# From unit 12 on, k and r are turned by VectorE in blocks of 32 and put in place by DMAs

## The chip, the cores and the metric

The kernel runs on one core of one Trainium2 chip. A core has the engines TensorE (PE in the profile, with its weight loads as PEld), VectorE (DVE), ScalarE (ACT), GpSimd (POOL) and SyncE (SP, which here only issues DMAs), and 16 DMA engines. SBUF is the on-chip memory of 128 partitions; PSUM is where TensorE writes. The metric is device time in microseconds of one execution; lower is better.

## The reference

Inputs are r, k and v of shape (batch 4, heads 8, positions 768, head size 48), a decay w and a bonus u per head and channel, and three feed-forward weights. All is 32-bit floating point.

```
for t in range(768):
    y[t]  = r[t] @ (state + (u * k[t]) outer v[t])      # per batch and head
    state = w * state + k[t] outer v[t]
x   = y, laid out as (4*768, 8*48) = (3072, 384)
g   = x @ w_gate            # 384 -> 1536
out = (g * sigmoid(g) * (x @ w_val)) @ w_out            # 1536 -> 384
```

## The kernel before

**Units.** The 3072 tokens are cut into 24 units of 128 tokens. Unit i is chunk c = i // 4 of batch b = i % 4, so four neighbouring units are the same chunk of the four batches. For a unit the recurrence becomes matrix products. k times powers of the decay is khat and r times their inverse is rhat; the product of the two, turned so that channels lie on the partitions (kT and rT), gives a 128x128 score per head. A mask keeps the scores of earlier positions, the bonus term stands on the diagonal (At), and the outputs are At times v plus rT times the state Z that the earlier chunks left. The update adds khat times v to Z.

**The steps of a unit.** `load` and `load_v` fetch k, r and v through SP's queue. `scale(i)` makes khat and rhat on POOL (L289, L293), and `own_product` the bonus products there (L211, L212), summed by DVE in `own_sum` (L217). `turn(i)` is eight transposes on PE, for the four pairs of heads of khat and then of rhat, into PSUM (L322), and two ACT copies to SBUF, kT (L324) and rT (L327). `diagonal` writes At on ACT (L309), `scores` runs PE (L335) and two masked copies on DVE (L340), `outputs` runs PE (L365) and an ACT copy into xT (L369), `update` PE (L378), DVE (L391) and POOL (L392).

**Buffers.** khat has four buffers (unit i uses i % 4), rhat two (i % 2), each of 128 partitions x 8 heads x 64 columns, of which 48 hold data and 16 zeros. kT has two, rT three. xT keeps the x of NX = 12 units in a ring.

**The feed-forward part.** Units are handled in groups of four by `four_units`: sums of x and of weights are made beforehand, so that 11 products per column block f do the work of more (L580, accumulators c_a and c_b in PSUM). The steps p1, p6 and p7 copy c_a to SBUF buffers of the ring "part" by ACT (L587, named p, u2 and u3), and DVE (L589 to L596) and POOL (L540 to L543, L564) combine them into hT. `two_projections` then multiplies hT by w_out (L474), and ACT issues the output stores (L497). These products are cut into some 40 pieces a group.

**The order.** It is written out by hand: each engine executes its instructions in the order in which the program names them, and semaphores are set for every dependence. The loop over stages s holds, in this order: own_sum(s); scale(s+1), own_product(s+1), load_v(s+1), load(s+3); turn(s); pieces; scores(s-1); from stage 12 on outputs(s-2); pieces; pieces; diagonal(s); pieces; update(s-2); pieces. `gaps(s, n)` feeds the pieces: from stage 12 on a stage takes its share of what is queued, at most 14, and divides it over the five places. A new group is queued every fourth stage, so a stage takes between 3 and 14 pieces.

**The names that matter here.** `scale_k`, `scale_r`, `turn`, `scores`, `outputs`, the ring "part" (pool `seven`), xT with NX, and the loop over s (L757 on).

Of the kernel before, what the change touches and what calls it, by code (L numbers as in the profile page):

```python
# [9 lines left out]
FP32 = mybir.dt.float32  # L10
# [5 lines left out]
P = 128  # L16
# [6 lines left out]
def fast(  # L23
# [25 lines left out]
    B, H, S, D = r.shape  # L49
    D2 = 2 * D  # L50
    VW = 2 * D + 16
    HP = H // 2
    R2 = 64 + D
    NCH = S // P
    N = B * NCH
# [3 lines left out]
    cst = ctx.enter_context(tc.tile_pool(name="cst", bufs=1))  # L59
    one = ctx.enter_context(tc.tile_pool(name="one", bufs=1))  # L60
    two = ctx.enter_context(tc.tile_pool(name="two", bufs=2))
    three = ctx.enter_context(tc.tile_pool(name="three", bufs=3))
    seven = ctx.enter_context(tc.tile_pool(name="seven", bufs=7))
    ps_a = ctx.enter_context(tc.tile_pool(name="ps_a", bufs=4, space=bass.MemoryType.PSUM))
    ps_w = ctx.enter_context(tc.tile_pool(name="ps_w", bufs=1, space=bass.MemoryType.PSUM))
    ps_f = ctx.enter_context(tc.tile_pool(name="ps_f", bufs=2, space=bass.MemoryType.PSUM))
# [7 lines left out]
    rscale = cst.tile([P, H, D], FP32, name="rscale")  # L74
# [9 lines left out]
    wg = cst.tile([P, CC, DFF], FP32, name="wg")  # L84
    wv = cst.tile([P, CC, DFF], FP32, name="wv")
    wo = cst.tile([P, FC, DM], FP32, name="wo")
    NX = 12
    xT = cst.tile([P, NX, CC, P], FP32, name="xT")
    Z = [cst.tile([P, HP, D2], FP32, name=f"Z{b}") for b in range(B)]
    r_ld = [cst.tile([P, H, D], FP32, name=f"r_ld{i}") for i in range(2)]  # L90
# [2 lines left out]
    v_ld = [cst.tile([P, HP, VW], FP32, name=f"v_ld{i}") for i in range(4)]  # L93


    khat = [cst.tile([P, H, 64], FP32, name=f"khat{i}") for i in range(4)]
    rhat = [cst.tile([P, H, 64], FP32, name=f"rhat{i}") for i in range(2)]
    At = [cst.tile([P, H, P], FP32, name=f"At{i}") for i in range(2)]
    kT = [cst.tile([P, HP, P], FP32, name=f"kT{i}") for i in range(2)]

    def load(i):
        c, b = divmod(i, B)
# [117 lines left out]
    sg0 = two.tile([P, 1], FP32, name="sg0", tag="sg0")  # L220
    for t in v_ld:
        dve.memset(t[:, :, D:64], 0.0)
    for t in khat + rhat:
        dve.memset(t[:, :, D:64], 0.0)
    dve.memset(wcol[:], 1.0)
    for e in range(2):
        sp.dma_start(out=wcol[64 * e : 64 * e + D, :], in_=w.rearrange("(a e) d -> e d a", e=2)[e])
# [57 lines left out]
    turned = {}  # L285
    small = deque()

    def scale_k(i):
        pool.tensor_mul(khat[i % 4][:, :, 0:D], k_ld[i % 2][:], kscale[:])  # L289

    def scale_r(i):
        for h in (slice(0, HP), slice(HP, H)) if i == 0 else (slice(0, H),):
            pool.tensor_mul(rhat[i % 2][:, h, 0:D], r_ld[i % 2][:, h], rscale[:, h])  # L293

    def scale(i):
        scale_k(i)
# [21 lines left out]
    def turn(i):  # L318
        for nm, t in (("kT", khat[i % 4]), ("rT", rhat[i % 2])):
# [5 lines left out]
            else:  # L325
                turned[i] = three.tile([P, HP, P], FP32, name=nm, tag=nm)
                act.copy(turned[i][:], tp[:])  # L327

    def scores(i):

        ps = [ps_a.tile([P, HP, P], FP32, name="s_ps", tag="a") for _ in range(2)]
        for a in range(HP):
            for e in range(2):
                rows = slice(64 * e, 64 * e + D)
                pe.matmul(  # L335
                    ps[e][:, a, :], kT[i % 2][rows, a, :], turned[i][rows, a, :],
                    start=True, stop=True, skip_group_check=True,
                )
        for e in range(2):
            dve.copy_predicated(  # L340
                At[i % 2][:].rearrange("p (a e) t -> p a e t", e=2)[:, :, e],
                mask[:].bitcast(INT32).unsqueeze(1).to_broadcast([P, HP, P]), ps[e][:],
            )

    def outputs(i):

        c, b = divmod(i, B)
        A, vl, z = At[i % 2], v_ld[i % 4], Z[b]  # L350
        rT = turned.pop(i)
        ps = ps_a.tile([P, CC, P], FP32, name="y_ps", tag="a")
        cols = [[] for _ in range(4)]
        for m in range(4 * CC):
            (cc, q), (a, s) = divmod(m, 4), divmod(m, 3)
            each = [(z[0:R2, a, 32 * s : 32 * s + 32], rT[0:R2, a, :])] if c > 0 else []
            if s < 2:
                each.append((vl[:, a, 32 * s : 32 * s + 32], A[:, 2 * a, :]))
            if s > 0:
                each.append((vl[:, a, 32 * s + 16 : 32 * s + 48], A[:, 2 * a + 1, :]))  # L360
            cols[q] += [(cc, x, n == 0, n == len(each) - 1) for n, x in enumerate(each)]
        for n in range(len(cols[0])):
            for q in range(4):
                cc, x, start, stop = cols[q][n]
                pe.matmul(  # L365
                    ps[32 * q : 32 * q + 32, cc, :], *x,
                    start=start, stop=stop, skip_group_check=True,
                )
        act.copy(xT[:, i % NX, :, :], ps[:])  # L369

# [82 lines left out]
    def project(g, n):  # L453

        h11, h12, h21, h22 = h_quarters(g)
        x = part_of.setdefault(g, {})
        if n == 0:
            one_bank = ps_f.tile([P, 2, 2 * P], FP32, name="o_f", tag="gv")[:, 0, 0:NH]
            if g % 2 == 0:
                x["a"] = ps_o.tile([P, 2 * P], FP32, name="o_a", tag="o")[:, 0:NH]  # L460
                x["b"] = one_bank
            else:
                x["a"] = one_bank
                x["b"] = ps_w.tile([P, 2 * P], FP32, name="o_b", tag="w_mag")[:, 0:NH]
            x["out"] = [two.tile([P, DM], FP32, name=n, tag=n) for n in ("o_sb1", "o_sb2")]
        lhs, rhs, acc = (
            (h11, w11, "a"), (h12, w21, "b"), (1, wt[0], "a"), (2, wt[1], "a"),
            (0, w12, "b"), (h22, wt[2], "a"), (3, w22, "b"),
        )[n]
        if isinstance(lhs, int):  # L470
            lhs = x["s"][lhs]
        ps = x[acc]
        for f in range(FH):
            pe.matmul(  # L474
                ps, lhs[:, f, :], rhs[:, f, :],
                start=(f == 0 and n in (0, 1, 4)), stop=(f == FH - 1), skip_group_check=True,
            )
        o1, o2 = x["out"]
        if n in (0, 2, 3):
            nm = {0: "p1", 2: "u2", 3: "u3"}[n]  # L480
            x[nm] = seven.tile([P, 2 * P], FP32, name=nm, tag="part")[:, 0:NH]
            act.copy(x[nm], ps)
        elif n == 1:
            dve.tensor_add(o1[:, 0:NH], x["p1"], ps)
        elif n == 5:
            act.copy(o2[:, 0:NH], ps)
        elif n == 6:
            dve.tensor_add(o1[:, NH:DM], x["u2"], ps)  # L488
        if n in (3, 4):
            if "c22" in x:  # L490
                dve.tensor_add(o2[:, NH:DM], x["u3"], x["b"])
            x["c22"] = True
        if n >= 5:
            j = 6 - n
            c, b = divmod(2 * g + j, B)
            n0 = S * b + P * c
            act.dma_start(out=out[n0 : n0 + P, :], in_=x["out"][j][:])  # L497
# [47 lines left out]
    def four(g, f, what):  # L545
# [37 lines left out]
        )  # L583
        if what in ("p1", "p6", "p7"):
            nm = {"p1": "p1", "p6": "u2", "p7": "u3"}[what]
            x[nm, f] = seven.tile([P, 2 * P], FP32, name=nm, tag="part")
            act.copy(x[nm, f][:], ps)  # L587
        elif what == "c11":
            dve.tensor_add(h[0], x.pop(("p1", f))[:], ps)  # L589
        elif what == "c21":  # L590
            dve.tensor_mul(h[0], h[0], x.pop(("sg0", f))[:])
            dve.tensor_mul(h[0], h[0], ps)
        elif what == "c22":
            dve.tensor_add(x["u3", f][:], x["u3", f][:], ps)  # L594
        elif what == "c12":
            dve.tensor_add(h[1], x.pop(("u2", f))[:], ps)  # L596
# [59 lines left out]
    def gaps(s, n):  # L656

        if s not in EARLY:
            if n == 0:
                share[0] = min(-(-len(todo) // (4 - (s - 9) % 4)), 14)  # L660
            feed(share[0] // 5 + (n < share[0] % 5))
            return
        for what in EARLY[s][n]:
            if what == "R":
                if done["pool"] < NW:
                    round_weights()
                elif len(summed) < 4:
                    weight_sum()
            else:
                feed(1)  # L670

    share = [0]
    LATE = 12
    EARLY = {s: ("" if s < 7 else "R", "F", "R", "F", "RF") for s in range(5, 12)}
    EARLY[4] = ("R", "F", "", "F", "F")
# [81 lines left out]
    for s in range(4, N + 2):  # L757
        if 4 < s < N:
            own_sum(s)
        if s + 1 < N:  # L760
            scale(s + 1)
            own_product(s + 1)
            load_v(s + 1)
            if s + 3 < N:
                load(s + 3)
        if s < N:
            turn(s)
        gaps(s, 0)
        if 4 <= s - 1 < N:
            while small:  # L770
                small.popleft()()
            scores(s - 1)
            if s >= LATE:
                outputs(s - 2)
            gaps(s, 1)
        gaps(s, 2)
        if s - 2 >= 4 and (s < LATE or s > N):
            outputs(s - 2)
        if s >= 5 and s % 2:
            queue((s - 3) // 2)  # L780
        if s < N:
            diagonal(s)
        if s - 2 >= 4:
            gaps(s, 3)
            update(s - 2)
        gaps(s, 4)
        if s == 12:
            n_ps = ps_a.tile([P, HP, P], FP32, name="n_ps", tag="a")
            pe.matmul(n_ps[0:1, 0, 0:1], badc[:], ones[:], start=True, stop=True)
            act.copy(outside, n_ps[0:1, 0, 0:1])  # L790
# [417 lines left out]
```

## Time and profile before

| What | Value |
|---|---|
| Median of 3 runs | 655.1 us (655.0 to 655.13) |
| Profiled execution, its own time | 655.57 us |
| Its span, first to last instruction | 653.5 us |
| Granted TensorE clock, mean | 0.996 |
| PE, PEld busy | 98%, 88% of the span |
| DVE, ACT, POOL busy | 53%, 39%, 46% |
| Turns on PE, units 0 to 23 | 192, from 13.9 to 459.2 us |
| The turns of units 12 to 23 begin at | 140.4, 169.5, 189.1, 227.5, 261.3, 292.4, 309.1, 346.0, 373.8, 412.6, 424.5, 458.4 us |
| ACT copies of turns, kT and rT | 24 of 578 ns and 24 of 593 ns |

A line of the groups reads: line of the kernel, engine, operation, what it writes and reads, shape, count, busy us, mean ns. The timeline has the start in us, the duration of a merged run of instructions, and what they are; an entry in brackets is the idle time of the engine ahead of it and what ended that. The durations of matmuls overlap, so their cost is read from start to start.

### The profile page before, as it was taken

What the parts mean: (1) busy time and instruction counts of PE and PEld (TensorE: products, weight loads), DVE (VectorE), ACT (ScalarE), POOL (GpSimd) and SP (SyncE); (2) the same over time, 40 slices, a digit from 0 to 9 for tenths busy, and PEclk for the clock granted to TensorE, in tenths of its full rate; (3) what the DMA queues carried; (4) which work ended last, traced back from release to release, by engine and by line L of the source; (5) the groups of instructions that cost most, each with busy time, mean ns of one, the idle gap of its engine ahead of it and who ended that gap; (6) DMA issues with size and microseconds to landing.
All of it is one profiled execution on the core that took longest, in us unless ns stands there. A gap on an engine that the chain in (4) does not pass through costs nothing.

```text
span 653.5 us, 11994 instructions
## 1 busy us (share of the span) xinstructions
PE 637.3 (98%) x4702; PEld 575.2 (88%) x4702; DVE 348.8 (53%) x711; ACT 257.4 (39%) x686; POOL 300.2 (46%) x333
## 2 busy tenths in 40 slices
PE   8899998999999999999999999999999999999996
PEld 8787877899988889988889988889988889988896
DVE  6668888364365556256548145546245546255460
ACT  4557776431344431344432244451244430234310
POOL 5968777961854430836416534641334310534110
PEclk9899999999999999999999999999999999999999
DMA  8969784221210010201101210000000000100001
GB/s 192 253 151 214 224 212 98 41 38 39 70 38 1 14 25 24 62 13 38 25 1 38 60 26 2 13 14 2 25 26 1 0 2 12 38 0 2 2 1 53
DMA packets 85779, 34.10 MB, mean 52 GB/s; under 512 B 76369, under 2 KB 79569, under 8 KB 85713
## 3 DMA queue, kind: packets, MB, share of 16 engines
q1 hardware_dynamic: 82256, 28.52, 19.0%
q10 hardware_dynamic: 3456, 4.72, 2.0%
q8 instruction: 39, 0.64, 0.4%
q14 instruction: 28, 0.22, 0.1%
HBM read 28.51 MB, written 4.72 MB: 51 GB/s over the span
## 4 chain that ended last, share of the span: by engine, by line
PE 86%; DVE 8%; ACT 4%; issue 1%; DMA 0%; SPq 0%; DVEq 0%; ACTq 0%
PE c_b L580 24%; PE c_a L580 20%; PE o_f L474 13%; PE o_a L474 7%; PE o_b L474 5%; PE y_ps L365 5%; PE gv L403 4%; PE s_ps L335 3%; PE tp L322 2%; PE u_ps L378 2%; ACT At L309 2%; DVE At L340 1%; DVE wo L184 1%; PE warm L245 1%; DVE hT L411 1%
## 5 line engine op out<-in xcount | busy, mean ns | idle before, releaser
L564 POOL TENSOR_TENSOR hT<-hT,u 128x256 f32<-128x256 f32 x60 | 47.3, 788 | 187.9 <-DVE hT L563 160.9
L587 ACT COPY u<-c_a 128x256 f32<-128x256 f32 x120 | 44.6, 371 | 87.0 <-PE c_a L580 86.9
L580 PE MATMUL c_a<-t,wv 128*128 128x256 f32 x240 | 72.0, 382 | 0.2 <-ACT u L587 0.2
L580 PE MATMUL c_b<-xT,wg 128*128 128x256 f32 x240 | 71.7, 380 | 0.0
L560 ACT ACTIVATE sg<-hT 128x256 f32<-128x256 f32 x120 | 50.0, 417 | 50.5 <-DVE hT L589 31.5
L309 ACT ACTIVATE At<-ident,du 128x128 f32<-128x128 f32 x184 | 64.3, 397 | 9.4 <-DVE o_sb L488 7.7
L594 DVE TENSOR_TENSOR u<-u,c_b 128x256 f32<-128x256 f32 x60 | 25.3, 421 | 70.4 <-PE c_b L580 64.1
L580 PE MATMUL c_b<-xT,s 128*128 128x256 f32 x240 | 61.6, 379 | 0.0
L589 DVE TENSOR_TENSOR hT<-p,c_b 128x256 f32<-128x256 f32 x60 | 25.2, 421 | 48.7 <-ACT u L587 24.4
L580 PEld LDWEIGHTS c_b<-xT,s 128*128 128x128 f32 x240 | 45.2, 190 | 6.6 <-DVE u L594 0.3
L540 POOL TENSOR_TENSOR s<-wv,wg 128x256 f32<-128x256 f32 x24 | 17.6, 733 | 72.4 <-PE o_f L474 57.1
L580 PEld LDWEIGHTS c_a<-t,wv 128*128 128x128 f32 x240 | 44.6, 190 | 7.1 <-ACT u L587 1.2
L580 PEld LDWEIGHTS c_b<-xT,wg 128*128 128x128 f32 x240 | 45.0, 190 | 6.1 <-issue 0.4
L340 DVE COPY_PREDICATED At<-mask,s_ps 128x512 f32<-128x512 int32 x48 | 33.0, 744 | 26.2 <-ACT At L309 16.0
L403 PE MATMUL gv<-xT,wg 128*128 128x256 f32 x144 | 36.8, 392 | 3.4 <-DVE hT L411 3.4
L365 PE MATMUL y_ps<-At,v_ld 128*32 128x128 f32 x768 | 36.1, 278 | 2.8 <-DVE At L340 2.8
L580 PE MATMUL c_b<-t,s 128*128 128x256 f32 x120 | 36.2, 383 | 0.0
L596 DVE TENSOR_TENSOR hT<-u,c_b 128x256 f32<-128x256 f32 x60 | 25.2, 421 | 20.1 <-PE c_b L580 19.9
L580 PE MATMUL c_b<-xT,wv 128*128 128x256 f32 x120 | 35.9, 381 | 0.0
L580 PE MATMUL c_a<-t,s 128*128 128x256 f32 x120 | 35.8, 380 | 0.0
L580 PE MATMUL c_a<-xT,wg 128*128 128x256 f32 x120 | 35.8, 380 | 0.0
L580 PE MATMUL c_a<-xT,wv 128*128 128x256 f32 x120 | 35.7, 379 | 0.0
(133 smaller groups left out, 1425.7 us busy)
## 6 DMA issues: line engine op xcount, KB each, us to landing
k_ld<-in_k_dram SPq DMA_DIRECT2D x24, 192.0 KB, 3.6
r_ld<-in_r_dram SPq DMA_DIRECT2D x24, 192.0 KB, 3.8
w_bits<-in_moe_w_gate_dram SPq DMA_DIRECT2D x6, 768.0 KB, 6.2
v_ld<-in_v_dram SPq DMA_DIRECT2D x48, 96.0 KB, 3.1
w_bits<-in_moe_w_val_dram SPq DMA_DIRECT2D x6, 768.0 KB, 6.5
w_bits<-in_moe_w_out_dram SPq DMA_DIRECT2D x6, 768.0 KB, 4.5
out_dram<-o_sb ACTq DMA_DIRECT2D x24, 192.0 KB, 1.9
ub<-in_u_dram SPq DMA_DIRECT2D x1, 192.0 KB, 4.1
```

The costliest lines, as they stand in the source:

```text
L309: lambda h=h: act.activation(At[i % 2][:, h, :], ident[:], AF.Identity, scale=du[:, h : h + 1])
L340: dve.copy_predicated(At[i % 2][:].rearrange("p (a e) t -> p a e t", e=2)[:, :, e], mask[:].bitcast(INT32).unsqueeze(1).to_broadcast([P, H ...
L365: pe.matmul(ps[32 * q : 32 * q + 32, cc, :], *x, start=start, stop=stop, skip_group_check=True,)
L403: pe.matmul(gv[:, o, :].rearrange("p (i t) -> p i t", i=2), wt[:, c, P * f : P * (f + 1)], xT[:, 2 * g % NX : 2 * g % NX + 2, c, :], start ...
L474: pe.matmul(ps, lhs[:, f, :], rhs[:, f, :], start=(f == 0 and n in (0, 1, 4)), stop=(f == FH - 1), skip_group_check=True,)
L560: act.activation(x[what, f][:], h[j], AF.Sigmoid)
L564: pool.tensor_mul(h[1], h[1], x.pop(("u3", f))[:])
L580: pe.matmul(ps.rearrange("p (i t) -> p i t", i=2), lhs, rhs, start=first, stop=what not in ("p2", "p5", "p4", "p3"), skip_group_check=True,)
L587: act.copy(x[nm, f][:], ps)
L589: dve.tensor_add(h[0], x.pop(("p1", f))[:], ps)
L594: dve.tensor_add(x["u3", f][:], x["u3", f][:], ps)
L596: dve.tensor_add(h[1], x.pop(("u2", f))[:], ps)
```

## The change

From unit 12 on PE no longer turns khat and rhat. A full turn of a 128x128 matrix is done in two steps instead: DMAs inside SBUF move 32x32 blocks to their mirrored places (16 DMAs a unit, each with 32 partitions x 8 pairs x 32 columns, issued by SP), and DVE turns each 32x32 block where it lies, once for kT and once for rT, straight to SBUF. khat and rhat become slots of one tile `hats` with two more slots for the moved blocks. The slots are arranged so that the k and the r of a unit are neighbours; for that, from unit 12 on two neighbouring units share one rhat buffer (i % 4 // 2), and the pairs of heads of even units lie in reversed order, which `at` undoes in `scores` and `outputs`. The DMAs of unit s+1 and the DVE turn of unit s are named in stage s after the second group of pieces. To make room, xT keeps 10 units, and the ring "part" has six buffers.

```diff
-    seven = ctx.enter_context(tc.tile_pool(name="seven", bufs=7))
+    six = ctx.enter_context(tc.tile_pool(name="six", bufs=6))
...
-    NX = 12
+    NX = 10
...
-    khat = [cst.tile([P, H, 64], FP32, name=f"khat{i}") for i in range(4)]
-    rhat = [cst.tile([P, H, 64], FP32, name=f"rhat{i}") for i in range(2)]
+    hats = cst.tile([P, 8, H, 64], FP32, name="hats")
+    khat, rhat = [hats[:, n] for n in (0, 2, 3, 5)], [hats[:, n] for n in (1, 4)]
...
+    blocks = [hats[:, n].rearrange("p h x -> p (h x)") for n in (7, 6)]
...
-    for t in khat + rhat:
-        dve.memset(t[:, :, D:64], 0.0)
+    dve.memset(hats[:, 0:6, :, D:64], 0.0)
...
+    def rhat_of(i):
+        return rhat[i % 2 if i < BLOCKS else i % 4 // 2]
+
+    def at(i, a):
+        return HP - 1 - a if i >= BLOCKS and i % 2 == 0 else a
...
+    def move_blocks(i):
+        h = hats[:].rearrange("p n h x -> p (n h x)")
+        first, step = ((0, 1), (11, -1), (12, 1), (23, -1))[i % 4]
+        for m in range(4):
+            for q in range(4):
+                src = h[32 * q : 32 * q + 32, P * first + 32 * m : P * first + 32 * m + 1]
+                dst = h[32 * m : 32 * m + 32, P * 31 + 32 * q : P * 31 + 32 * q + 1]
+                sp.dma_start(
+                    out=bass.AP(
+                        tensor=dst.tensor, offset=dst.offset,
+                        ap=[list(dst.ap[0]), [-P, 2 * HP], [1, 32]],
+                    ),
+                    in_=bass.AP(
+                        tensor=src.tensor, offset=src.offset,
+                        ap=[list(src.ap[0]), [P * step, 2 * HP], [1, 32]],
+                    ),
+                )
+
+    def turn_blocks(i):
+        turned[i] = three.tile([P, HP, P], FP32, name="rT", tag="rT")
+        for dst, src in ((kT[i % 2], blocks[0]), (turned[i], blocks[1])):
+            dve.transpose(dst[:].rearrange("p a t -> p (a t)"), src)
...
-                    ps[e][:, a, :], kT[i % 2][rows, a, :], turned[i][rows, a, :],
+                    ps[e][:, a, :], kT[i % 2][rows, at(i, a), :], turned[i][rows, at(i, a), :],
...
+    BLOCKS = 12
...
-        if s < N:
+        if s < BLOCKS:
             turn(s)
...
             gaps(s, 1)
+        if BLOCKS <= s < N:
+            turn_blocks(s)
+        if BLOCKS <= s + 1 < N:
+            move_blocks(s + 1)
         gaps(s, 2)
```

More of the change, by code (lines that the diff above doesn't have):

```diff
@@ L292, in scale_r @@
         for h in (slice(0, HP), slice(HP, H)) if i == 0 else (slice(0, H),):
-            pool.tensor_mul(rhat[i % 2][:, h, 0:D], r_ld[i % 2][:, h], rscale[:, h])
+            pool.tensor_mul(rhat_of(i)[:, h, 0:D], r_ld[i % 2][:, h], rscale[:, h])
     def scale(i):
@@ L355, in outputs @@
             (cc, q), (a, s) = divmod(m, 4), divmod(m, 3)
-            each = [(z[0:R2, a, 32 * s : 32 * s + 32], rT[0:R2, a, :])] if c > 0 else []
+            each = [(z[0:R2, a, 32 * s : 32 * s + 32], rT[0:R2, at(i, a), :])] if c > 0 else []
             if s < 2:
@@ L480, in project @@
             nm = {0: "p1", 2: "u2", 3: "u3"}[n]
-            x[nm] = seven.tile([P, 2 * P], FP32, name=nm, tag="part")[:, 0:NH]
+            x[nm] = six.tile([P, 2 * P], FP32, name=nm, tag="part")[:, 0:NH]
             act.copy(x[nm], ps)
@@ L585, in four @@
             nm = {"p1": "p1", "p6": "u2", "p7": "u3"}[what]
-            x[nm, f] = seven.tile([P, 2 * P], FP32, name=nm, tag="part")
+            x[nm, f] = six.tile([P, 2 * P], FP32, name=nm, tag="part")
             act.copy(x[nm, f][:], ps)
```

## The prediction

> **What bounds the kernel now.** I read the page first: busy time by engine, then the chain that ended last. The columns of the first line are busy us, share of the span, instructions.
>
> ```profile
> PE 637.3 (98%) x4702; PEld 575.2 (88%) x4702; DVE 348.8 (53%) x711; ACT 257.4 (39%) x686; POOL 300.2 (46%) x333
> ...
> PE 86%; DVE 8%; ACT 4%; issue 1%; DMA 0%; SPq 0%; DVEq 0%; ACTq 0%
> PE c_b L580 24%; PE c_a L580 20%; PE o_f L474 13%; PE o_a L474 7%; PE o_b L474 5%; PE y_ps L365 5%; PE gv L403 4%; PE s_ps L335 3%; PE tp L322 2%; PE u_ps L378 2%; ACT At L309 2%; DVE At L340 1%; DVE wo L184 1%; PE warm L245 1%; DVE hT L411 1%
> ```
>
> TensorE carries the chain, and the turns (tp) are 2% of it. A share is an average, so I took the table of busy time in stretches, one per stage from stage 12 on (columns: length, PE, weight load, DVE, ACT, POOL, granted clock).
>
> ```profile
> 189.00:228.00 39.00, 39.00 (x251) 34.07 (x250) 22.39 (x50) 17.75 (x50) 21.22 (x27) 1.00 0.10 19
> 292.00:309.00 17.00, 17.00 (x147) 14.87 (x146) 11.53 (x21) 7.54 (x21) 11.24 (x15) 1.00 0.16 32
> 413.00:425.00 12.00, 12.00 (x125) 10.51 (x124) 6.39 (x14) 5.31 (x15) 7.08 (x9) 1.00 0.00 1
> ```
>
> PE fills every such stretch; over 140 to 460 us its records leave 0.2 us idle. There a microsecond taken from PE is a microsecond of the kernel, unless a wait takes its place. Stages are unequal, 12 to 39 us, because the planner feeds different numbers of feed-forward pieces; this decides below.
>
> **What is removed.** The mean of 273 ns for a turn overlaps its neighbours, so I took the timeline of PE at unit 14's turn (start, us, then the group).
>
> ```profile
> 189.12 0.60 PE L322 MATMUL tp<-ident,khat 128*128 128x128 f32 x4
> 189.55 0.60 PE L322 MATMUL tp<-ident,rhat 128*128 128x128 f32 x4
> 189.99 0.60 PE L580 MATMUL c_b<-xT,wg 128*128 128x256 f32 x2
> ```
>
> From the first turn to the next product is 0.87 us; eleven of the twelve units from 12 on show 0.87, one 0.93. So 12 x 0.87 + 0.06 = **10.5 us** leave PE. ACT loses 24 copies of about 0.585 us (14 us); worth nothing, since PE does not wait for it here. Without this cover the gain would not exist at all: it is only PE's time that counts.
>
> **What is added, and its prices.** *DVE.* Two block turns of 128x512 per unit. The trace has none. [...] I take 0.69 because the masked copies of the same shape (L340) take 0.74. DVE is 53% busy and has room. The pair stands in DVE's program order behind the second group of pieces, and what is queued behind it are sums that free PE's accumulators. The tight one is L589: it runs from 302.57 to 302.99, 0.6 us before PE writes its accumulator again. A pair just ahead holds it up to 1.4 us less the idle 0.6 us, which costs PE up to 0.4 us. One unit in three or four meets that: 3 x 0.35 = **1.0 us**. Ends: 0, and 12 x 1.4 = 17 us if nothing were covered.
>
> *SP and the transfers.* 16 issues a unit, 32 KB each in 256 runs of 128 B, 192 issues in all. [...] q1's 82256 packets took 19.0% of 16 engines' 653.5 us, 24 ns each[...]. Issuing takes longer. From the source view of the v loads, minimum, median and maximum in ns, and the time to landing:
>
> ```profile
> L111 SPq DMA_DIRECT2D v_ld<-in_v_dram x48: 367/498/2253, 8.2 to 425.1; - x48
> ...
> DMA to landing us min/median/max: 2.0/3.1/6.5
> ```
>
> The first of a pair is 0.37, the second 0.50, and the first loads at start-up follow each other by 0.46 to 0.62. So 15 x 0.47 + 1.9 (the page's row of the output stores, from issue to landing) = 9.0 us from the first issue to the last landing. Call it X; bounds 7.5 (0.37 an issue) and 14 (every issue as slow as 0.58, with 0.2 of waits between and landing 2 us). [...] in the trace's wait fields loads and stores take eight completion semaphores in turn and each waits for the one before on its own. Eight issues span 3.8 us against some 2 us of landing, so that adds nothing inside a unit.
>
> **Where it waits.** move_blocks(s+1) needs scale(s+1), done at the top of stage s, and turn_blocks(s), since it overwrites the blocks. So it starts in mid-stage and has until the next mid-stage: 12 us or more, above X, so DVE does not wait. Loads queue behind it on SP for up to 7 us; they are wanted a stage or two later, so nothing.
>
> POOL does wait. For units from 12 on, two neighbours share one rhat buffer, so scale_r of odd i must wait until move_blocks(i-1) has landed, and those have only the rest of a stage. What is queued behind it on POOL is seen in its timeline at the top of stage 14:
>
> ```profile
> 189.94 0.99 POOL L293 TENSOR_TENSOR rhat<-r_ld,rscale 128x384 f32<-128x384 f32 x1
> 190.90 0.99 POOL L211 TENSOR_TENSOR rk<-r_ld,k_ld 128x384 f32<-128x384 f32 x1
> 191.97 1.07 POOL L212 TENSOR_TENSOR rk<-rk,ub 128x384 f32<-128x384 f32 x1
> 192.99 0.73 POOL L564 TENSOR_TENSOR hT<-hT,u 128x256 f32<-128x256 f32 x1
> ```
>
> L564 releases a "part" buffer, ACT fills it next with a copy of c_a, and PE needs that copy before it adds to c_a again. By the wait fields buffers are handed out in the order of their release: with seven, the u2 copies wait for POOL; with six it is the next copy, p, at 194.16 here. It starts 0.44 us after L564 ends (2.3 us usually), and PE has 0.6 us more; the turn taken away brings it 0.87 us nearer. So six buffers alone cost nothing, but a late POOL reaches PE. Unit by unit:
> - 15: moves start about 183.0 (stage 13's second group ends near 181.2, the pair follows), scale_r is due at 189.94, so it is X-6.9 late; PE stalls X-6.9 + 0.87 - 0.44 - 0.6 = X-7.1.
> - 19: moves start 303.5, due 309.72; L564 would end at 313.54, its copy is due 315.4 plus 0.6; PE stalls X-8.7.
> - 23: moves start 422.9, due 427.29; the copy comes late, at 436.77 before; PE stalls X-9.8.
> - 13, 17, 21: X-7.7, none, X-11 late, in stages where the copies have 2 us or more.
> At X = 9.0: 1.9 + 0.3 = **2.2 us**.
>
> *ACT.* Its output stores share the eight semaphores. A store behind the moves can wait for a move and hold ACT: the stores at 160.4, 162.4, 275.3 and 364.1 lie near moves. If the shared semaphore's last holder is an early move the cost is 0, if a late one some 4 us at 275.3, where products follow. I take **0.5 us**.
>
> *The rest.* x for 10 units: a slot is rewritten ten units on, and the group that reads it has then been through PE for a stage or more: 0. One memset of 768 columns replaces six of 128 (165 ns): 0. The reversed order of pairs (at) changes addresses only. [...]
>
> **The sum.** Profiled span 653.5 - 10.5 + 1.0 + 2.2 + 0.5 = 646.7 us. The profiled execution took 655.57, 2.07 around its span, and the median of the runs is 655.1, 0.47 below; so 646.7 + 1.6 = 648.3, and I say **648.5 us**.
>
> **Rivals.**
> - *A, the sum above*: 645.5 to 652. For it: PE full, X computed from issue rows.
> - *B, all hidden*: X at 7.5 and the DVE pair in gaps; 655.1 - 10.5 + 0.4 = 645.0. Against it: the short stages 13 and 21.
> - *C, the transfers become the bound through POOL, slower than before*: the stalls are 3X - 25.6, and with 1.5 for the rest they reach 10.5 at X = 11.5; at 13.5 the time is 655.1 - 10.5 + 1.5 + 14.9 = 661.0. This needs 0.64 us an issue, or a wait between DMAs that the trace does not show. For it: r loads hold SP 0.58, and 128 B runs between partitions are in no row. Against it: those r loads follow 1024 runs, these 256.
> - *D, ACT held by shared semaphores[...]*: 3 x 2.5[...] = 8 us on top of 2; 652 to 657. That scale_k or the updates wait for moves because all lie in one tile would give the same; against it, xT is one tile too and PE read it at 320.75 while ACT still wrote another part.
>
> **Chances.** A 0.46, B 0.12, C 0.27, D 0.15. The measurement can tell 0.2%, about 1.3 us. A and B are faster; D splits in thirds; C is slower: faster 0.63, same 0.05, slower 0.32. A's own range is 645.5 to 652; for 8 in 10 the range takes in B and C up to X = 13.5: 644.5 to 661.5.
>
> **What the next profile shows.** Right: tp only to unit 11; PE still over 97% busy; 192 more issues on SP at about 0.47; turns near 0.7 us; POOL L293 waiting for a DMA at the tops of stages 12, 14, 18 and 22, by 2, 3 and 5 us in the last three, and PE idle after ACT copies of c_a in 14. Wrong: moves over 11 us from first issue to landing, DVE waiting for a DMA at the turns, ACT waiting at a store, or an idle PE at other tops than these.

## The result and the profile after

The changed kernel takes **644.52 us** (median of 6 runs, 643.26 to 645.14) against 654.92 us before (median of 6, 654.05 to 655.13): ratio 0.984, interval 0.9828 to 0.9853. The forecast was 648.5 us; the gain is 10.4 us instead of 6.6. The time lies where rival B stood (645.0), below the range of the sum itself (645.5 to 652) and at the very edge of the wide one (644.5 to 661.5).

The page of the changed kernel, in the order in which the page of before was read: span, busy us by engine (share, instructions), the chain that ended last by engine and by line, the group of `scale_r` on POOL (busy us, mean ns | idle before it and what ended it), the DMA queue q1 (packets, MB, share of 16 engines), and the new DMA issues (KB each, us to landing).

```profile
span 641.6 us, 12075 instructions
...
PE 625.3 (97%) x4606; PEld 563.7 (88%) x4606; DVE 361.6 (56%) x730; ACT 245.1 (38%) x662; POOL 300.2 (47%) x333
...
q1 hardware_dynamic: 134480, 34.82, 25.7%
...
PE 83%; DVE 8%; ACT 4%; issue 2%; DMA 1%; SPq 1%; POOL 0%; DVEq 0%; ACTq 0%
PE c_b L615 24%; PE c_a L615 20%; PE o_f L509 13%; PE o_a L509 7%; PE o_b L509 6%; PE y_ps L400 5%; PE gv L438 3%; PE s_ps L370 3%; ACT At L318 2%; PE u_ps L413 2%; DVE wo L187 1%; DVE hT L446 1%; DMA w_bits<-in_moe_w_gate_dram 1%; DVE sg L445 1%; DVE wo L188 1%
...
L302 POOL TENSOR_TENSOR hats<-r_ld,rscale 128x384 f32<-128x384 f32 (+1 forms) x25 | 25.0, 1001 | 24.1 <-DMA hats<-hats 24.1
...
hats<-hats SPq DMA_DIRECT2D x192, 32.0 KB, 2.0
```

PE has 96 instructions fewer and 12.0 us less of busy time in this execution; tp is no longer among the lines of the chain. DVE has 12.8 us more, and POOL now waits 24.1 us for the moves. Yet PE is still busy 97% of a shorter span. Lines have moved: L580 is now L615, L587 is L622, L564 is L599, L293 is L302; the moves are L347, the block turns L362.

The table of busy time in stretches, for the same three stages as in the prediction (each stretch shorter by about the turn that is gone; columns as there):

```profile
185.60:223.70 38.10, 37.99 (x239) 32.99 (x238) 21.98 (x50) 16.81 (x48) 21.27 (x27) 1.00 0.26 43
286.30:302.40 16.10, 16.10 (x138) 13.89 (x138) 12.28 (x22) 6.23 (x19) 11.16 (x15) 1.00 0.23 40
403.80:414.90 11.10, 11.10 (x116) 9.61 (x115) 7.54 (x16) 4.31 (x13) 6.92 (x9) 1.00 0.05 7
```

PE fills the stages as it did: over 140 to 460 us its records leave 0.21 us idle, against 0.2 before. The timeline of PE at the place of unit 14's turn shows the seam closed, 0.43 us from start to start:

```profile
185.36 0.59 PE L615 MATMUL c_a<-xT,wv 128*128 128x256 f32 x2
185.79 0.59 PE L615 MATMUL c_b<-xT,wg 128*128 128x256 f32 x2
```

Where the gain arises is seen when one product is followed through both traces, the first product of a unit's outputs (y_ps), in us from the start of the span. The second execution is the run e0 below, of the same kernel.

| y_ps, before | after | later or earlier | e0_changed | later or earlier |
|---|---|---|---|---|
| 78.14 | 76.54 | -1.60 | 77.69 | -0.45 |
| 133.28 | 131.66 | -1.62 | 132.84 | -0.44 |
| 148.31 | 145.82 | -2.50 | 147.00 | -1.31 |
| 236.91 | 232.13 | -4.77 | 232.98 | -3.93 |
| 353.89 | 345.64 | -8.25 | 346.49 | -7.40 |
| 466.31 | 454.48 | -11.83 | 455.33 | -10.97 |
| 527.15 | 515.32 | -11.83 | 516.18 | -10.97 |

Between 133.28 and 466.31 the distance grows by 10.21 us in one execution and 10.53 us in the other, and neither before nor after. From one stage to the next it grows by 0.8 to 1.0 us; only once, in the first execution ahead of the y_ps at 232.13, it is 0.5. The constant 1.6 or 0.44 us lies at the start-up, differs between two executions of one kernel, and is not the change's. So the twelve turns are gained whole in e0_changed; in the other execution 0.3 us is given back at one place, which is shown under e3.

### The profile page after: what moved, and what is told of

Its sections match the earlier page's. It is cut to its first block, busy times and chain, and to the rows that moved or that the text cites. A ratio compares the mean times of both kernels' runs of the same rounds, so it can differ in the third digit from the quotient of the medians.

```text
span 641.6 us, 12075 instructions
## 1 busy us (share of the span) xinstructions
PE 625.3 (97%) x4606; PEld 563.7 (88%) x4606; DVE 361.6 (56%) x730; ACT 245.1 (38%) x662; POOL 300.2 (47%) x333
## 4 chain that ended last, share of the span: by engine, by line
PE 83%; DVE 8%; ACT 4%; issue 2%; DMA 1%; SPq 1%; POOL 0%; DVEq 0%; ACTq 0%
PE c_b L615 24%; PE c_a L615 20%; PE o_f L509 13%; PE o_a L509 7%; PE o_b L509 6%; PE y_ps L400 5%; PE gv L438 3%; PE s_ps L370 3%; ACT At L318 2%; PE u_ps L413 2%; DVE wo L187 1%; DVE hT L446 1%; DMA w_bits<-in_moe_w_gate_dram 1%; DVE sg L445 1%; DVE wo L188 1%
## 5 line engine op out<-in xcount | busy, mean ns | idle before, releaser
L599 POOL TENSOR_TENSOR hT<-hT,u 128x256 f32<-128x256 f32 x60 | 47.5, 793 | 162.2 <-DVE hT L598 135.2
L622 ACT COPY u<-c_a 128x256 f32<-128x256 f32 x120 | 44.5, 371 | 87.2 <-PE c_a L615 86.9
L615 PE MATMUL c_a<-t,wv 128*128 128x256 f32 x240 | 72.2, 382 | 0.1
L615 PE MATMUL c_b<-xT,wg 128*128 128x256 f32 x240 | 71.7, 380 | 0.0
L615 PE MATMUL c_b<-xT,s 128*128 128x256 f32 x240 | 61.6, 379 | 0.0
L615 PEld LDWEIGHTS c_b<-xT,s 128*128 128x128 f32 x240 | 45.3, 190 | 6.6 <-DVE u L629 0.2
L615 PEld LDWEIGHTS c_a<-t,wv 128*128 128x128 f32 x240 | 44.7, 190 | 7.0 <-ACT u L622 1.1
L615 PEld LDWEIGHTS c_b<-xT,wg 128*128 128x128 f32 x240 | 45.2, 190 | 6.2 <-issue 0.4
L624 DVE TENSOR_TENSOR hT<-p,c_b 128x256 f32<-128x256 f32 x60 | 25.1, 419 | 42.9 <-PE c_b L615 39.9
L615 PE MATMUL c_b<-t,s 128*128 128x256 f32 x120 | 36.2, 383 | 0.1
L302 POOL TENSOR_TENSOR hats<-r_ld,rscale 128x384 f32<-128x384 f32 (+1 forms) x25 | 25.0, 1001 | 24.1 <-DMA hats<-hats 24.1
L627 DVE TENSOR_TENSOR hT<-hT,c_a 128x256 f32<-128x256 f32 x60 | 25.3, 421 | 19.1 <-PE c_a L615 18.0
L615 PE MATMUL c_b<-xT,wv 128*128 128x256 f32 x120 | 35.9, 381 | 0.0
L615 PE MATMUL c_a<-t,s 128*128 128x256 f32 x120 | 35.8, 380 | 0.0
```

The lines of the kernel that those rows point to most:

```text
L599: pool.tensor_mul(h[1], h[1], x.pop(("u3", f))[:])
L615: pe.matmul(ps.rearrange("p (i t) -> p i t", i=2), lhs, rhs, start=first, stop=what not in ("p2", "p5", "p4", "p3"), skip_group_check=True,)
```

## The experiments

Two theories stood at first. **H**: the gain is PE's time of the 96 turns, and everything added is hidden. **K**: the additions cost about what was forecast (3.7 us), and some other part of the change, the single tile, the six buffers or x for ten units, gains as much. Each edit is made to the changed kernel; ratios are against the kernel before.

| Run | Edit | us | Ratio, interval |
|---|---|---|---|
| e0_changed | none | 644.38 | 0.9839 (0.9826 to 0.9853) |
| e1_pe_turns | PE turns all units | 655.13 | 1.0004 (0.9995 to 1.0012) |
| e2_no_turns | no turn at all from unit 12 | 645.77 | 0.986 (0.9845 to 0.9875) |
| e6_act_copies | ACT's 24 copies are back | 645.54 | 0.9863 (0.9847 to 0.9878) |
| e3_dve_twice | block turns doubled | 650.45 | 0.9931 (0.9917 to 0.9944) |
| e9_four_moves | 4 moves a unit | 645.93 | 0.9861 (0.9846 to 0.9876) |
| e5_part5 | ring "part" with 5 | 646.20 | 0.9866 (0.9852 to 0.988) |
| e4_half_moves | 32 moves a unit | 676.94 | 1.0345 (1.033 to 1.036) |
| e7_blocks8 | from unit 8 on | 652.56 | 0.9967 (0.9954 to 0.998) |
| e8_blocks8_two_queues | the same, two queues | 663.87 | 1.0129 (1.0114 to 1.0145) |

**e1_pe_turns.** The one tile, x for ten units and the six buffers stay; PE turns all units.

```diff
-    BLOCKS = 12
+    BLOCKS = 24
```

> BLOCKS = 24: PE turns all units again, no transfers and no turns on VectorE; the one tile for khat and rhat, x for 10 units and six part buffers stay. Theory H (the gain is PE's 12 x 0.87 us and all that was added is hidden): ratio to before 1.000, within 0.2%. Rival K (the additions cost the 3.7 us of the prediction and something else gains as much, the buffers and the layout among the candidates): ratio 0.995 or 1.003 and beyond.

655.13 us, ratio 1.0004. Busy time of its page:

```profile
PE 635.8 (97%) x4702; PEld 573.6 (88%) x4702; DVE 348.4 (53%) x706; ACT 258.2 (40%) x686; POOL 300.4 (46%) x333
```

The rest of the change is worth nothing, in either direction, to within 0.12%. K falls: there is no second gain that could hide a cost.

**e2_no_turns.** From unit 12 on nobody turns: units use the kT and rT of earlier ones, so a part of the computation is left out.

```diff
+            kept = turned[s]
...
-            turn_blocks(s)
-        if BLOCKS <= s + 1 < N:
-            move_blocks(s + 1)
+            turned[s] = kept
```

> From unit 12 on nothing is turned at all: no transfers, no turns on VectorE, none on PE; units 12 to 23 use the kT and rT of earlier units, so that part of the computation is left out. H: the additions cost nothing, so leaving them out gives the changed kernel's ratio, 0.984 within 0.002. K: without 3.7 us of waits the ratio is 0.978 to 0.980.

645.77 us; its interval, 0.9845 to 0.9875, overlaps that of the changed kernel. With no block turns, no moves and no waits of POOL for them the kernel isn't faster.

One thing in e2 is new, though, and it costs time. In stage 14 POOL has nothing to wait for and makes rhat at once, and an operation of DVE with two inputs in SBUF takes 2.04 us instead of 0.41. PE waits for what stands behind it. DVE's timeline of e2, then PE's:

```profile
188.05 2.04 DVE L598 TENSOR_TENSOR hT<-hT,sg 128x256 f32<-128x256 f32 x1
190.02 0.41 DVE L624 TENSOR_TENSOR hT<-p,c_b 128x256 f32<-128x256 f32 x1
```

```profile
190.47 0.70 PE L615 MATMUL c_b<-t,s 128*128 128x256 f32 x2 [0.68 <-DVE hT L624]
```

The same operation of DVE in the changed kernel, where POOL is waiting for the moves at that time:

```profile
186.80 0.41 DVE L598 TENSOR_TENSOR hT<-hT,sg 128x256 f32<-128x256 f32 x1
```

It takes 2.04 to 2.05 us in the four kernels in which POOL computes there (before, e1, e2 and e9), and 0.41 to 0.42 us in the eight in which POOL stands waiting. In the kernel before, PE doesn't wait for it. Followed by y_ps as in the table above, e2 gains 9.67 us, and this stage gains 0.02 where it gains 0.96 in the changed kernel. Without this loss of 0.94 us e2 gains 10.6 us, e0_changed 10.5. So all additions together cost nothing that can be told, and POOL's wait in stage 14 even spares PE a wait, which the prediction did not foresee.

**e6_act_copies.** Two ACT copies of 128x512 a unit are put back where the old ones stood.

```diff
+    def act_copies(i):
+        turned[i] = three.tile([P, HP, P], FP32, name="rT", tag="rT")
+        for dst in (kT[i % 2], turned[i]):
+            act.copy(dst[:], ident[:].unsqueeze(1).to_broadcast([P, HP, P]))
...
-        turned[i] = three.tile([P, HP, P], FP32, name="rT", tag="rT")
...
+        elif s < N:
+            act_copies(s)
```

> At the place of the removed turns ScalarE again makes two copies of 128x512 a unit (of the identity, into the tiles that VectorE then overwrites), 14 us in all. H: 0.984 within 0.002. K: part of the gain was ScalarE's relief, so 0.987 or more.

645.54 us, again an overlapping interval: 13.0 us more busy time on ACT (258.1 against 245.1) cost 1.0 to 1.2 us by the medians. The trace has nearly all of it at one place: at 368.67 us PE waits 1.14 us for an ACT copy of c_a, where the changed kernel waits 0.10. The kernel before had all its copies and waited 0.20 there. So some 0.1 us of the gain may be ACT's, no more. Why the copies cost more in e6 than in the kernel before wasn't tried; in e6 they go into tiles that DVE writes right after them.

**e3_dve_twice.** Every block turn is issued twice.

```diff
             dve.transpose(dst[:].rearrange("p a t -> p (a t)"), src)
+            dve.transpose(dst[:].rearrange("p a t -> p (a t)"), src)
```

> VectorE turns each unit's blocks twice: 24 more instructions, 1.4 us a unit more on VectorE. H: 0.984 to 0.986, PE idle between 140 and 460 us still under 1 us. K with the prediction's term (1 us of PE stall a 12 pairs, growing when the block is 2.8 us long): 0.989 or more, with PE idle before products that wait for VectorE.

650.45 us, some 6 us more than the changed kernel; PE's records leave 4.22 us idle over 140 to 460 us. So K's forecast for this run came, and H's (under 1 us idle) didn't: the prediction's mechanism for DVE is real, only its cover is larger than thought. The tightest place in the changed kernel, in DVE's timeline (start, us, then the instruction):

```profile
204.22 0.70 DVE L362 STREAM_TRANSPOSE kT<-hats 128x512 f32<-128x512 f32 x1
204.85 0.66 DVE L362 STREAM_TRANSPOSE rT<-hats 128x512 f32<-128x512 f32 x1
205.44 0.37 DVE L624 TENSOR_TENSOR hT<-p,c_b 128x256 f32<-128x256 f32 x1
```

PE's timeline at that place:

```profile
205.16 0.60 PE L615 MATMUL c_a<-t,s 128*128 128x256 f32 x2
205.87 0.70 PE L615 MATMUL c_b<-t,s 128*128 128x256 f32 x2
```

The same place of PE's timeline with doubled turns (in brackets the idle time and what ended it; the line numbers of e3 are one higher):

```profile
207.24 0.59 PE L616 MATMUL c_a<-t,s 128*128 128x256 f32 x2
209.25 0.70 PE L616 MATMUL c_b<-t,s 128*128 128x256 f32 x2 [1.42 <-DVE hT L625]
```

c_b can be written again when L624 has read it. In the changed kernel PE comes there 0.11 us early (205.76 to 205.87); the second pair makes it 1.42 us, 1.31 more for two more turns of 0.7 us. At this place a single pair just fits, with nothing left: in this execution the products come 0.3 us later by it, in e0_changed not at all.

The idle time of PE's records is less than the loss, because the records overlap: a product of 128x256 is recorded as 0.38 us, and the next starts 0.22 us after it. By an estimate from these two numbers and the waits that follow, a wait of up to some 0.17 us shows no idle time, and a longer one shows that much too little. Four waits of e3 count 4.07 us as idle and delay the products by 4.8; five shorter ones count 0.05 and delay them by 0.9. Followed by y_ps, e3 gains 4.6 us instead of 10.5, so all of the 6 us is lost in these stages.

**e9_four_moves.** Four transfers of 128 partitions take the place of sixteen of 32; blocks don't change their quarter of partitions, so that part of the computation is left out.

```diff
-        for m in range(4):
-            for q in range(4):
-                src = h[32 * q : 32 * q + 32, P * first + 32 * m : P * first + 32 * m + 1]
-                dst = h[32 * m : 32 * m + 32, P * 31 + 32 * q : P * 31 + 32 * q + 1]
+        for q in range(4):
+            src = h[:, P * first + 32 * q : P * first + 32 * q + 1]
+            dst = h[:, P * 31 + 32 * q : P * 31 + 32 * q + 1]
```

> Four transfers a unit instead of sixteen, each over all 128 partitions: the same bytes and the same 128 B runs, but the blocks stay in their quarter of the partitions, so k and r of units 12 to 23 are not turned rightly; that part of the computation is left out. If the queue is held by the number of issues, the moves take 4 to 5 us instead of 12 and GpSimd's waits of 5 to 8 us for them are gone. H (those waits reach nobody at six part buffers): the time is that of the changed kernel beside it, within 0.2%. K: they cost something, and 0.5% or more is gained. If the moves still take 12 us, bytes or runs set their time and not the issues.

645.93 us. The moves of a unit take 5.4 to 6.5 us instead of 11.7 to 13.1, and POOL's waits go from 24.1 us in four to 1.9 us in one:

```profile
POOL hats L302 <- DMA hats<-hats: 1.9, 1, 1.9
```

The time doesn't fall; it is 1.5 us above e0_changed, and 0.94 of that is lost where e2 loses it, with the same 2.04 us of DVE's L598 (L596 in e9) and 0.68 us of PE's waiting. So POOL's 24.1 us of waiting cost nothing, and shorter moves alone win nothing.

**e5_part5.** The ring that was to carry POOL's lateness to PE has one buffer fewer.

```diff
-    six = ctx.enter_context(tc.tile_pool(name="six", bufs=6))
+    six = ctx.enter_context(tc.tile_pool(name="six", bufs=5))
```

> Five part buffers instead of six. If buffers are bound in the order of their release, as the prediction had it, a late GpSimd reaches PE through them: with five the copies come 2 to 7 us too early in stages 14, 18 and 22 and PE stalls 5 us or more, ratio 0.992 or more. If a copy takes whichever buffer is free and no more than five are held at once, PE stays full except perhaps where GpSimd waits for the moves: 0.984 to 0.988.

646.20 us, 1.7 us above the changed kernel by the medians, with intervals that just overlap. Followed by y_ps, e5 gains 8.6 us instead of 10.2 or 10.5, so the loss is real. The time lies in the range of the second theory (0.984 to 0.988), but the chain that the prediction drew appears in stages 14, 18 and 22, though small. A line of the view of waits of e5 (us in total, times, longest):

```profile
ACT u L622 <- POOL hT L599: 6.3, 3, 2.8
```

PE's timeline where one of those copies comes late:

```profile
431.55 0.70 PE L615 MATMUL c_a<-t,s 128*128 128x256 f32 x2 [0.63 <-ACT u L622]
```

**e4_half_moves.** The same blocks in 32 transfers of 16 KB a unit instead of 16 of 32 KB.

```diff
+                for n in (0, HP):
+                    f, l = P * (first + step * n) + 32 * m, P * (31 - n) + 32 * q
...
-                        ap=[list(dst.ap[0]), [-P, 2 * HP], [1, 32]],
+                            ap=[list(dst.ap[0]), [-P, HP], [1, 32]],
...
-                        ap=[list(src.ap[0]), [P * step, 2 * HP], [1, 32]],
+                            ap=[list(src.ap[0]), [P * step, HP], [1, 32]],
```

> Each transfer is cut into two of half the blocks: 32 issues a unit instead of 16, the same bytes. If an issue holds the queue 0.65 us whatever its size, the moves of a unit take about 23 us instead of 12: scale_r of units 13, 15, 19 and 23 waits some 10 us longer (15 to 18 us), VectorE waits about 5 us for the blocks of unit 22 in stage 22 and others stay covered. H: the cover then ends in the short stages, PE stalls 5 to 20 us, ratio 0.99 to 1.015. If the issue time halves with the size: the moves still take 12 us and the ratio is 0.984. Rival of the prediction (stalls of 3X - 25.6): at X = 23, 43 us, ratio 1.05.

676.94 us, 32 more than the changed kernel, and slower than before. An issue still takes 0.64 us (0.65 in the changed kernel), so a unit's moves last 22.4 to 23.7 us. The ratio lies above H's range (0.99 to 1.015) and below the rival's 1.05. Both mechanisms that the prediction feared now show, and a third, which the expectation of this run names. The view of waits of e4:

```profile
POOL hats L302 <- DMA hats<-hats: 78.0, 6, 18.5
...
ACT u L623 <- POOL hT L600: 19.2, 3, 8.0
...
PE c_a L616 <- ACT u L623: 18.5, 7, 6.7
...
ACT At L318 <- DMA hats<-hats: 15.6, 4, 7.1
```

POOL is late, ACT waits for POOL's L600, and PE for ACT's copy. And ACT is held at an output store by a move, 7.1 us the longest, in ACT's timeline of e4:

```profile
174.83 0.34 ACTq L533 DMA_DIRECT2D out_dram<-o_sb  x1
175.22 0.40 ACT L318 ACTIVATE At<-ident,du 128x128 f32<-128x128 f32 x1 [7.12 <-DMA hats<-hats]
```

PE's two waits right behind that, at 176.07 and 180.74, are 2.43 and 2.71 us; those through POOL, at 212.21 and 337.59, 5.42 and 6.71. The third is DVE waiting for a unit's moves before its turn, in stage 22, and PE behind it:

```profile
459.74 0.71 DVE L363 STREAM_TRANSPOSE kT<-hats 128x512 f32<-128x512 f32 x1 [5.81 <-DMA hats<-hats]
```

```profile
461.40 1.21 PE L616 MATMUL c_b<-xT,s 128*128 128x256 f32 x4 [3.83 <-DVE u L630]
```

From 140 us to the end PE has 22.4 us more idle time than in the changed kernel, and 7.7 us more busy time (633.0 against 625.3, at a mean granted clock of 0.986 against 0.999): 30.1 of the 30.3 us by which the span is longer.

**e7_blocks8.** The new way four units earlier, which takes four more turns from PE (0.97 us each in the trace of before, 3.9 us).

```diff
-    BLOCKS = 12
+    BLOCKS = 8
```

> VectorE turns from unit 8 on (BLOCKS = 8). PE loses four more turns of 0.97 us, 3.9 us, in stages of 13 to 14 us in which moves of 12 us must fit and VectorE also rounds weights. H without new waits: ratio 0.978 to 0.980. With waits of VectorE or GpSimd for moves that last as long as the stage: 0.984 to 0.995.

652.56 us, 8 us slower than the changed kernel, and a little more than either theory allowed (0.9967). The moves of units 8 to 11 take 12.6 to 12.8 us. In the kernel before, stages 9 to 11 last 14.3, 12.6 and 12.0 us from turn to turn, and between two turns both the moves and the turn itself must fit. Now DVE is the one that waits, 0.33, 4.95 and 8.94 us for units 9, 10 and 11. DVE's timeline of e7 in stage 11:

```profile
143.76 0.71 DVE L362 STREAM_TRANSPOSE kT<-hats 128x512 f32<-128x512 f32 x1 [8.94 <-DMA hats<-hats]
144.40 0.67 DVE L362 STREAM_TRANSPOSE rT<-hats 128x512 f32<-128x512 f32 x1
```

And PE's behind it:

```profile
145.98 4.18 PE L509 MATMUL o_f<-wo,hT 128*128 128x192 f32 x12 [3.32 <-DVE hT L446]
```

**e8_blocks8_two_queues.** As e7, with half the moves of units 8 to 11 issued by ACT, to shorten them.

```diff
-                sp.dma_start(
+                (act if i < 12 and q % 2 else sp).dma_start(
...
-    BLOCKS = 12
+    BLOCKS = 8
```

> VectorE turns from unit 8 on, and for units 8 to 11 every second transfer is issued from ScalarE's queue instead of SyncE's. If the waits of 5 and 9 us of VectorE for the moves in stages 10 and 11 came from SyncE's string of issues, they are gone with half the string, and the four turns' 3.9 us come out: ratio 0.978 to 0.981. Rival: ScalarE, held by its issues and by its wait for VectorE's turn, keeps PE waiting instead: 0.985 to 0.997.

663.87 us, slower than before and than both forecasts. The moves of units 9 to 11 do get shorter (6.9 to 8.9 us; unit 8's, the first, still took 12.9), and DVE no longer waits for a move. But ACT computes, and it is held by its issues. The source view of the moves in e8 counts the two queues (ns, minimum, median, maximum):

```profile
L347 SPq DMA_DIRECT2D hats<-hats x224: 590/609/1676, 83.9 to 461.7; - x112
L347 ACTq DMA_DIRECT2D hats<-hats x32: 597/623/1694, 79.8 to 147.3; - x32
```

ACT's timeline of e8 shows the price:

```profile
103.89 6.74 ACTq L347 DMA_DIRECT2D hats<-hats  x8
110.67 0.51 ACT L169 ACTIVATE w_mag<-w_bits 128x384 f32<-128x384 f32 x1 [9.71 <-DMA hats<-hats]
```

The 9.71 us in which ACT computed nothing hold the 6.74 us of its eight issues and 2.9 us ahead of them. DVE needs w_mag next, and PE had stood idle for 7.40 us when its gv products went on at 114.13.

**e0_changed.** The changed kernel once more, beside e8 and e9.

> The changed kernel itself, beside the next two. H: ratio 0.984 to 0.986, PE idle 0.2 us between 140 and 460 us.

644.38 us, ratio 0.9839, as in the first comparison, and PE idle for 0.10 us. None of the variants is faster.

## Why the prediction was wrong

**What leaves PE: right.** 12 x 0.87 + 0.06 = 10.5 us was forecast, 10.4 was measured between the medians, and 10.2 and 10.5 in the traces of two executions. e1, e2 and e6 show that it is this and, but for some 0.1 us, nothing else. What went wrong is the other side of the sum: 1.0 for DVE, 2.2 for POOL and 0.5 for ACT, 3.7 us in all, of which at most 0.3 came. Without them the forecast would have been 644.8.

**The price of a move: too low.** The forecast was 0.47 us an issue and X = 9.0 us from the first issue to the last landing. The source view of the moves in the changed kernel (ns, minimum, median, maximum; below, to landing in us):

```profile
L347 SPq DMA_DIRECT2D hats<-hats x192: 593/609/1657, 133.1 to 440.7; - x192
...
DMA to landing us min/median/max: 1.9/2.0/3.7
```

From start to start it is 0.65 us, and X is 11.7 to 13.1, about 12. The landing (1.9) was right for most units; in three the last move took 2.8 to 3.3 us to land. The mean over pairs of v loads was the wrong row: its first of a pair is 0.37, and no move takes so little. Nor does the size explain the difference: e4, the changed kernel and e9 show moves of 16 KB, 32 KB and 128 KB holding the queue about alike, 0.64, 0.65 and 0.72 us from start to start. The bound of 14 held X, but "moves over 11 us" was among the prediction's own signs of being wrong, and it came.

**POOL's wait: right, and 3 us longer for the same reason.** Waits of 2, 3 and 5 us were forecast at the tops of stages 14, 18 and 22; they are 5.17, 5.52 and 7.81, which is 3.2, 2.5 and 2.8 more, as X is 2.7 to 3.2 longer there; stage 12's is 5.56. No more than 0.2 us of it reaches PE.

**The failed step: what becomes of POOL's lateness.** The forecast was that with six buffers the next copy, p, takes the buffer that L564 (now L599) releases, so that PE stalls X - 7.1 in stage 14, X - 8.7 in 18 and X - 9.8 in 22. At X = 12 that law gives 10.4 us, all of the gain. So it was luck that the forecast lay only 4 us too high: X too small hid most of what the law would have claimed. With the right X the same sum gives 648.5 - 2.2 + 10.4 = 656.7 us, slower than before. I had extended "in the order of their release" from the wait fields of a kernel with seven buffers to one with six. POOL's timeline of the changed kernel at the top of stage 14:

```profile
191.82 1.00 POOL L302 TENSOR_TENSOR hats<-r_ld,rscale 128x384 f32<-128x384 f32 x1 [5.17 <-DMA hats<-hats]
192.79 0.99 POOL L214 TENSOR_TENSOR rk<-r_ld,k_ld 128x384 f32<-128x384 f32 x1
193.86 1.01 POOL L215 TENSOR_TENSOR rk<-rk,ub 128x384 f32<-128x384 f32 x1
194.82 0.74 POOL L599 TENSOR_TENSOR hT<-hT,u 128x256 f32<-128x256 f32 x1
```

ACT's timeline there, of which the copies of c_a are shown:

```profile
189.94 0.37 ACT L622 COPY p<-c_a 128x256 f32<-128x256 f32 x1 [0.37 <-PE c_a L615]
...
191.61 0.37 ACT L622 COPY u<-c_a 128x256 f32<-128x256 f32 x1 [1.00 <-PE c_a L615]
...
193.33 0.37 ACT L622 COPY u<-c_a 128x256 f32<-128x256 f32 x1 [0.35 <-PE c_a L615]
...
197.59 0.37 ACT L622 COPY p<-c_a 128x256 f32<-128x256 f32 x1 [0.67 <-PE c_a L615]
...
199.37 0.37 ACT L622 COPY u<-c_a 128x256 f32<-128x256 f32 x1 [1.41 <-PE c_a L615]
```

The copy p of the prediction is the one at 189.94: it starts 4.9 us before the late L599 does. By the wait fields it waits for PE and ACT alone, as the next three wait for PE alone; the first copy that waits for POOL again is the fifth, u at 199.37. L599 ends at 195.56 and has 3.8 us to spare there, though it is 5.2 us late. PE doesn't wait after ACT's copies in stage 14, which the prediction had named as a sign of being right. In e4, whose program differs only in the moves, that very copy is the one that stops, as ACT's timeline shows:

```profile
203.80 0.37 ACT L623 COPY p<-c_a 128x256 f32<-128x256 f32 x1 [0.67 <-PE c_a L616]
211.78 0.37 ACT L623 COPY u<-c_a 128x256 f32<-128x256 f32 x1 [7.61 <-POOL hT L600]
```

This gives the law its right constants. POOL's wait in stage 14 is 15.21 us in e4, 10.04 more; less 3.81 to spare and the 0.6 that PE has behind a copy (the prediction's figure), 5.6 us should reach PE, and 5.42 did. In stage 18 the wait is 15.87 instead of 5.52, and L599 has 2.60 us to spare (312.78 to the copy at 315.38): 10.35 - 2.60 - 0.6 = 7.15, and 6.71 did. So by this estimate PE would stall in the changed kernel from X of about 16.6 (12.2 + 3.8 + 0.6) in stage 14 and 14.9 (11.7 + 2.6 + 0.6) in stage 18, not from 7.1 and 8.7. Stage 22 is the closest: there L599 ends at 429.00, the copy that waits for it starts at 429.33, and PE would stall from X of 12.2 + 0.3 + 0.6 = 13.1. In e7 unit 22's moves take 12.6 us; the same copy then waits 0.52 us for POOL, and PE doesn't wait, as the estimate says. An X just above 13.1 wasn't tried. e4 doesn't try it either: in its wait fields the copy at this place (453.94) doesn't wait for POOL at all, so even the number of moves changes which copy gets which buffer. How the buffers are handed out stays open; the wait fields show only the outcome.

**DVE: the price right, the cost not.** 0.69 us a turn was forecast, the author's estimate beside the 0.74 of the masked copies of the same shape, and the trace has at most 0.71 (kT) and 0.67 (rT). 1.0 us of cost was forecast at three places like L589. At the tightest one PE waits 0.11 us, 0.3 counting the overlap of its records, in one execution and not at all in the other; e3 shows the cover ending within the second pair.

**ACT's stores: 0.5 forecast, nothing seen.** In the changed kernel ACT never waits for a move. That a move can hold a store is shown by e4 (7.12 us at one store), where a unit's moves last twice as long.

**The rest: right, but for one thing.** x for ten units, the memset, `at` and the shared tile cost nothing (e1). Moves in flight didn't slow the one operation that was compared: from stage 12 on DVE's L624 takes 420 ns by the median, with a move in flight (18 of them) as without (42); for the other engines this was not shown. L624 has one input in SBUF, and its 60 instances in the changed kernel take 374 to 422 ns, with POOL at work beside it or not. L598 has two, and in stage 14 it took 2.04 us with POOL at work beside it (e2, e9) and 0.41 in the changed kernel, where POOL waited; so the change in POOL's waits changed DVE's time there, which the prediction didn't look at.

**The rivals.** B gave the right time for a wrong reason: X is 12, not 7.5, and all is hidden nonetheless. C set its break-even at X = 11.5 and was to decide by an issue of 0.64 us; the issue is 0.65, and nothing follows from it, since C rested on the failed step. D didn't come.

## What to carry to other kernels

A wait that appears on a helper engine is priced by the time that its next customer has to spare, and that is read at the buffer's actual next user in the wait fields; with another number of buffers the user is another one, so the old order can't be carried over. Where that can't be known ahead, the range should treat "reaches the bound" and "doesn't" as two cases rather than build a law on one. The same moves that are free in the changed kernel, where one unit's start 18 us or more after the last unit's, stop DVE for up to 8.94 us in e7, where turns fall due every 12 to 14 us. So how far such a change can be extended is decided by the stretches in which the moves and the turn don't both fit.

A variant that leaves work out can start a wait of its own, as e2 and e9 do. So its trace is read for new waits before its time is taken as the price of what was left out.

## What the runs showed of the hardware

- A move inside SBUF held SP's queue for 0.61 us by the median in the changed kernel (32 KB over 32 partitions), 0.65 from start to start, and for 0.60 and 0.64 in e4 (16 KB); e9's four of 128 KB over 128 partitions took 0.68 and 0.72. Splitting in two took a unit's moves from 11.7 to 13.1 us to 22.4 to 23.7 (e4). The landing took 1.9 to 3.7 us, 2.0 by the median; of some 12 us of a unit's moves in the changed kernel 15 issues are 9.8.
- The same issue on ACT's queue held ACT as long (0.62 us by the median), and eight of them held it 6.74 us, within 9.71 us in which it computed nothing (e8).
- A turn of 128x512 fp32 in 32x32 blocks took DVE 0.66 to 0.71 us in the changed kernel.
- An operation of DVE with two inputs in SBUF (L598, 128x256 fp32) took 2.04 to 2.05 us in the four kernels in which GpSimd was computing beside it in stage 14, and 0.41 to 0.42 us in the eight in which it stood still. Not every overlap lengthens it: in the kernel before (L563 there) the next one, at 195.36 us, took 0.42 beside L541 of GpSimd.
- In e2 a wait of PE of 0.68 us by its records delayed the product behind it by 0.84. In the changed kernel a product of 128x256 is recorded as 0.38 us and follows the one before it by 0.22; an estimate from these is that a wait of PE costs some 0.17 us more than the idle time of its records says.
- In e4 and e7, where PE's records leave 38.9 and 22.0 us of the span idle (16.3 in the changed kernel), the mean granted clock of the profiled execution was 0.986 and 0.987; in e8, where PE once stood idle for 7.40 us, it was 0.979, and in the others 0.995 to 1.0. Which causes which wasn't tried.
